# Probabilities transposed in 32x32 blocks by VectorE, and values summed over 32-key blocks in eight tiles of TensorE, in a fused attention and FFN kernel

## The chip, the cores and the metric

The kernel runs on one core of one Trainium2 chip. The metric is device time in microseconds, the median of several runs. The engines are named as in the profile: PE is TensorE (with PEld its weight loads), DVE is VectorE, ACT is ScalarE, POOL is GpSimd, SP is SyncE, which issues most DMAs.

## The reference

There are two parts, and the second takes the first one's output. Attention runs for 8 batches and 8 heads over 576 positions of 64 dimensions, causal by blocks of 64 positions. Its output, 4608 tokens by 512, goes through a bilinear FFN of width 1536.

```python
scores = scale * np.matmul(q, k.transpose(0, 1, 3, 2))
mask = block_i >= block_j            # blocks of 64 positions
scores = np.where(mask, scores, -1000000000.0)
scores = scores - np.max(scores, axis=-1, keepdims=True)
attn = np.exp(scores)
attn = attn / (np.sum(attn, axis=-1, keepdims=True) + 1e-09)
attn_out = np.matmul(attn, v)
...
x = np.ascontiguousarray(attn_out.transpose(0, 2, 1, 3)).reshape(B * S, H * D)
a = x @ w_a
b = x @ w_b
return (a * b @ w_out).astype(np.float32)
```

All inputs are float32. The kernel computes most matmuls as sums of products of float32r parts (a high and a low part of each operand, three products); those of the values, and the scores of the first six pairs, are plain float32.

## The kernel before, in words

Attention is done in 32 pairs of heads, `p`. One turn `s` of the loop at the end of the code below is a *slot*. It walks through the table `SLOT`, whose entries are (generator, pair relative to `s`, number of FFN matmuls that follow). `S1` is a step of `softmax` of pair `s`, `T1` a step of `turn` of pair `s - 1`, and `V_` is `values` of pair `s - 2`. `LAG` is 2, so the loop has two slots more than there are pairs. The FFN matmuls come from `first_pass`, which does 4 of the 12 chunks of the FFN's width for the tokens of batches whose attention is ready; `want` meters them out at 72 a slot, from `MOE_FROM` on, which counts half slots. PE's instructions stand in the order in which this loop emits them; those of the other engines are ordered by a scheduler. In the first slots, where no FFN matmul is ready, `KEEP` puts a few matmuls of zeros behind each step. After attention the other chunks follow in a second pass that this change does not touch.

In a pair, queries are taken in tiles of 128: tile `t` sees `nk[t]` keys, 192, 320, 448 and, for `LAST` = 3, 512. The first and the last block of 64 queries form a tile of their own, `NT` = 4, with 128 keys, the "side". `softmax` computes the scores of `LAST`, of the side and of tile 1 (L383), takes row maxima on DVE (L388, and `nb` at L411), and exponentials on ACT (L391), which also sums them; then scores (2, h) and (0, h) for both heads h, and the same for these. Line 434 makes the reciprocals `rc` of the sums, and POOL multiplies the exponentials by them in place (L438, ten operations a pair). The scores lie in banks of PSUM from a ring of four, `ps_sc`.

`turn` transposes the scaled exponentials on PE, 128 by 128 against an identity matrix, 28 a pair in seven groups (L457), each group into one of two banks `tp`; ACT copies each group to `ah` (L460). `values` multiplies: 12 matmuls a pair (L475) with 128 keys as the contraction, 64 columns of v as weights, one head in each half of the array's columns, sums in `av` and `av0` in the same two banks. DVE copies the sums to `xf` (L484, L485), and the parts `xh` and `xl` for the FFN are made from it. `load_v` loads v of a pair with two DMAs of 160 KB.

The functions that the change touches, and the loop that calls them, with the line numbers of the profile:

Of the kernel before, what the change touches and what calls it, by code (L numbers as in the profile page):

```python
# [26 lines left out]
MOE_FROM = 10.2  # L27
# [27 lines left out]
def attention_then_bilinear_ffn(  # L55
# [212 lines left out]
    ps_sc = psum(right, "ps_sc", 4)  # L268
    ps_t = psum(right, "ps_t", 1)

    ident = const.tile([P, P], F32, name="ident")
    make_identity(nc, ident)
# [14 lines left out]
    SC = slice(P * SIDE_T, P * SIDE_T + BLK), slice(P * SIDE_T + BLK, P * (SIDE_T + 1))  # L287
    NE = 4
    e_bufs, s_bufs = [], []
    for i in range(NE):  # L290
        es = [const.tile([P, ew[t]], F32, name=f"e{i}_{t}") for t in range(NT)]
        for t in range(LAST):
            nc.gpsimd.memset(es[t][:, nk[t]:], 0.0)
        e_bufs.append((es, const.tile([P, P], F32, name=f"e{i}_s")))
# [38 lines left out]
    def load_v(p):  # L333
        b, h, n = pair_of(p)
        vv = heads[p]["v"] = apool.tile([P, 2, NCH + 1, D], F32, tag="v", name=f"v{n}", bufs=3)
        for j in range(2):
            nc.sync.dma_start(vv[:, j], vm[b, h + j])
# [103 lines left out]
    def turn(p):  # L441

        n = pair_of(p)[2]
        heads[p]["a"] = ah = apool.tile([P, 2, NCH, W], F32, tag="ah", name=f"ah{n}")
        for t, hs in [(t, [h]) for t in range(LAST, 0, -1) for h in range(2)] + [(0, [0, 1])]:
            tp = ps_t.tile([P, 4, P], F32, tag="tp", name=f"tp{n}_{t}_{hs[0]}", bufs=2)
            m = min(t + 2, NCH)
            todo = []
            for h in hs:
                es, e_s = e_bufs[(2 * p + h) % NE]  # L450
                todo += [es[t][:, c * P:(c + 1) * P] for c in range(m)]
                if t == SIDE_T:
                    assert m == SIDE
                    todo.append(e_s)
            m = len(todo) // len(hs)
            for c, src in enumerate(todo):
                mark = nc.tensor.transpose(tp[:, c], src, ident)  # L457
            at = slice(hs[0], hs[-1] + 1), slice(m), slice(P * t, P * (t + 1))
            got = tp[:, :len(todo)].rearrange("p (h c) n -> p h c n", h=len(hs))
            nc.scalar.copy(ah[(slice(None), *at)], got)  # L460
            yield mark

    def values(p):
# [5 lines left out]
        av = ps_t.tile([P, W], F32, tag="tp", name=f"av{n}", bufs=2)  # L469
        av0 = ps_t.tile([P, 512], F32, tag="tp", name=f"av0{n}", bufs=2)[:, :BLK]  # L470
# [404 lines left out]
```

## Time and profile before

| what | value |
|---|---|
| median of 3 runs | 1278.81 us |
| runs | 1275.3 to 1279.34 us |
| the profiled execution, as timed | 1277.34 us |
| its span in the trace | 1275.5 us |
| busy: PE, DVE, ACT, POOL | 1229.0, 789.1, 622.8, 353.5 us |
| FFN matmuls start after | 113 us |
| attention ends at about | 650 us |

The profile was taken of one execution. Busy time is time in which an engine had an instruction under way; matmuls overlap, so their busy times are longer than the distance from one start to the next. A line of a group names the line of the kernel, the engine, the operation, output<-input, partitions x elements and the count, then its busy time and the mean of one in nanoseconds, then the idle time before it and what ended most of that.

### The profile page before, as it was taken

To read this page: it belongs to the slowest core of one execution; us is meant where nothing else is said; L and a number is where in the kernel's file an instruction comes from. 1 tells how busy PE (TensorE), PEld (TensorE's weight loads), DVE (VectorE), ACT (ScalarE), POOL (GpSimd) and SP (SyncE) were. 2 spreads that over 40 slices of the span, in tenths; PEclk is the share of its full clock that TensorE was granted. 3 is DMA by queue.
4 is the path that set the end of the run, shared out by engine and by line. 5 is a ranking of instruction groups with operands and counts; after the bars stand their busy time and mean duration, and the time that the engine had idled before them with its cause. 6 is when DMAs were issued, how large, how long until landed. Compare 5 with 4: busy or idle time off the path is not lost.

```text
span 1275.5 us, 22228 instructions
## 1 busy us (share of the span) xinstructions
PE 1229.0 (96%) x8132; PEld 1114.6 (87%) x8132; DVE 789.1 (62%) x1932; ACT 622.8 (49%) x1550; POOL 353.5 (28%) x540
## 2 busy tenths in 40 slices
PE   6789999999999999999999899999999999999998
PEld 4556778888888888888889799999999999999998
DVE  5875444345444454444538999778778677577664
ACT  3656667576675665766645444344344223123210
POOL 2453653554535545355330020120121000000000
PEclk7888999999999999999999999999999999999999
DMA  5342222222222223221133454563578542253131
GB/s 191 107 139 72 71 77 81 96 65 74 80 88 88 65 73 97 70 88 59 35 109 95 151 119 135 153 153 95 142 192 278 161 149 85 65 149 102 47 100 62
DMA packets 68652, 135.66 MB, mean 106 GB/s; under 512 B 7616, under 2 KB 42432, under 8 KB 68544
## 3 DMA queue, kind: packets, MB, share of 16 engines
q1 hardware_dynamic: 57024, 115.37, 28.2%
q0 software_dynamic: 6912, 9.44, 4.7%
q10 hardware_dynamic: 4608, 9.44, 2.2%
q8 instruction: 64, 1.05, 0.3%
q14 instruction: 44, 0.36, 0.1%
HBM read 87.03 MB, written 47.19 MB: 105 GB/s over the span
## 4 chain that ended last, share of the span: by engine, by line
PE 74%; ACT 12%; DVE 10%; issue 3%; DMA 1%; POOL 0%; SPq 0%; ACTq 0%; DVEq 0%
PE pso_z L727 15%; PE ps L223 9%; PE psw_z L681 8%; PE psx_z L681 8%; PE psv_z L681 7%; PE av L475 7%; PE pso L223 6%; PE tp L457 5%; PE s L383 5%; ACT e L391 5%; ACT ah L460 4%; PE psy_z L681 4%; DVE nm L388 3%; ACT e_s L391 2%; PE keep L586 1%
## 5 line engine op out<-in xcount | busy, mean ns | idle before, releaser
L223 PE MATMUL ps<-xh,wab 128*128 128x288 f32 x1024 | 228.8, 305 | 0.0
L727 PE MATMUL pso_z<-h_z,wo 128*128 128x384 f32 x1152 | 203.7, 334 | 2.1 <-DVE u_z L708 2.1
L727 PEld LDWEIGHTS pso_z<-h_z,wo 128*128 128x128 f32 x1152 | 200.2, 188 | 2.5 <-issue 2.3
L438 POOL TENSOR_SCALAR e<-e,rc 128x512 f32<-128x512 f32 (+3 forms) x256 | 150.7, 611 | 161.4 <-DVE rc L434 95.2
L223 PEld LDWEIGHTS ps<-xh,wab 128*128 128x128 f32 x1024 | 168.1, 188 | 8.5 <-issue 5.2
L223 PE MATMUL ps<-xl,wab 128*128 128x288 f32 x512 | 158.0, 309 | 0.0
L460 ACT COPY ah<-tp 128x512 f32<-128x512 f32 x224 | 133.5, 597 | 41.6 <-PE tp L457 41.1
L388 DVE TENSOR_REDUCE nm<-s 128x1 f32<-128x512 f32 (+4 forms) x320 | 147.0, 484 | 9.1 <-PE s L383 6.0
L383 PE MATMUL s<-k,q 64*128 64x512 f32 (+3 forms) x900 | 118.1, 367 | 27.4 <-ACT e L391 24.7
L112 ACT CAST h_z<-u_z 128x384 fp32r<-128x384 f32 x96 | 49.3, 513 | 175.8 <-DVE u_z L706 160.2
L457 PE MATMUL tp<-ident,e 128*128 128x128 f32 x832 | 130.8, 278 | 0.1
L383 PEld LDWEIGHTS s<-k,q 64*128 64x128 f32 x900 | 78.5, 190 | 59.5 <-ACT e L391 42.8
L790 POOL DMA_DIRECT2D part<-pt x48 | 42.7, 1038 | 287.1 <-ACT pt L789 286.4
L681 PE MATMUL psx_z<-xh,wab 128*128 128x384 f32 x384 | 117.6, 342 | 3.7 <-DVE u_z L699 2.0
L681 PE MATMUL psw_z<-xh,wab 128*128 128x384 f32 x384 | 117.4, 341 | 0.0
L681 PE MATMUL psv_z<-xh,wab 128*128 128x384 f32 x384 | 116.2, 338 | 0.0
L223 PE MATMUL pso<-hh,wo 128*128 128x288 f32 x480 | 112.5, 311 | 0.8 <-ACT a L247 0.8
L457 PEld LDWEIGHTS tp<-ident,e 128*128 128x128 f32 x832 | 105.6, 143 | 5.7 <-issue 2.5
L391 ACT ACTIVATE e<-s,nm 128x448 f32<-128x448 f32 (+2 forms) x192 | 101.3, 540 | 19.0 <-DVE nm L388 18.9
L484 DVE COPY xf<-av 128x512 f32<-128x512 f32 x32 | 22.1, 691 | 130.4 <-PE av L475 130.4
L475 PE MATMUL av<-ah,v 128*64 128x64 f32 (+4 forms) x768 | 93.6, 393 | 6.6 <-ACT ah L460 4.5
L223 PEld LDWEIGHTS ps<-xl,wab 128*128 128x128 f32 x512 | 96.4, 188 | 1.6 <-issue 0.4
(114 smaller groups left out, 2323.4 us busy)
## 6 DMA issues: line engine op xcount, KB each, us to landing
xr<-xd SPq DMA_DIRECT2D x48, 384.0 KB, 3.9
raww<-wab SPq DMA_DIRECT2D x24, 512.0 KB, 3.9
v<-vm SPq DMA_DIRECT2D x64, 160.0 KB, 3.4
xd<-xf ACTq DMA_DIRECT2D x32, 288.0 KB, 2.6
part<-ob SPq DMA_DIRECT2D x64, 144.0 KB, 2.0
part<-pt POOLq DMA_DIRECT2D x48, 192.0 KB, 7.3
pt<-part SPq DMA_DIRECT2D x48, 192.0 KB, 3.2
outT<-pt SPq DMA_DIRECT2D x48, 192.0 KB, 3.3
```

Source lines behind the costliest of these rows:

```text
L112: nc.scalar.copy(hi, src)
L223: mm = nc.tensor.matmul(ps, w_, d_, start=(i == 0), stop=(i == n - 1))
L383: mark = nc.tensor.matmul(outs[h], qq[r, q0[t]:q0[t] + P], keys, start=j == 0, stop=j == len(qk) - 1)
L388: nc.vector.tensor_reduce(nm[:, h, t:t + 1], view, axis=AX.X, op=ALU.max, negate=True)
L391: nc.scalar.activation(out, view, AF.Exp, bias=bias, accum_out=sm[:, h, t, :1])
L438: nc.gpsimd.tensor_scalar(ev, ev, rc[:, h, t:t + 1], 1.0, op0=ALU.mult, op1=ALU.mult)
L457: mark = nc.tensor.transpose(tp[:, c], src, ident)
L460: nc.scalar.copy(ah[(slice(None), *at)], got)
L475: mark = nc.tensor.matmul(out[r], v[:, i, c], a[:, i, src, cols], start=start, stop=stop, skip_group_check=True)
L681: nc.tensor.matmul(ps, wt[:, i, iw], j[:, ix], start=start and kp == 0 and i == 0 and j is xh, stop=kp == KP - 1 and i == 1, skip_group_ch ...
L727: nc.tensor.matmul(ps, wt[:, a, osl], b, start=i == 0, stop=i == 3 * len(fs) - 1)
L790: nc.gpsimd.dma_start(part[o * P:(o + 1) * P, ts], t, accum_op=ALU.add)
```

## The change

The identity matrix, `ps_t` and the transposes on PE go. `turn` now transposes with `nc.vector.transpose`, which turns each block of 32 by 32 in its place: 12 instructions a pair, over 3200 columns, into `at`, of which there is one buffer. So `at` holds, for each head, tile and key block of 32, keys on the partitions, but the four groups of 32 partitions are four groups of queries, and each group needs its own copy of v. The host lays v out four times, once for each group of 32 partitions, and `load_v` loads it in one DMA of 1152 KB a pair, two buffers in place of three.

`values` sums over 18 key blocks of 32: for each of them four row groups `i` of 32 partitions, and in each both heads in the two halves of the columns, 144 matmuls a pair in place of 12. Row group i of both heads sums into bank `av[i]`. These four banks come from `ps_sc`, which has six now. In the order of that ring `av[0]` and `av[1]` take the banks of tile 1 and the side, `av[2]` and `av[3]` those of (2, 0) and (2, 1); the next pair's first scores take those of (0, 0) and (0, 1). ACT copies the sums to `xf` in six copies; DVE has none.

`values` of pair s - 1 stands in slot s now, behind the sixth of `softmax`'s eight steps, that of (2, 1), with 14 FFN matmuls behind it, and 7 and 11 more behind the last two steps. `load_v`, `split_qk` and `load_qk` are called at other entries, `MOE_FROM` is 9.6, the loop has one slot more than there are pairs, and `KEEP` counts only at entries with FFN matmuls.

```diff
--- before.py
+++ after.py
@@ -4,7 +4,6 @@
 import concourse.bass as bass
 import concourse.tile as tile
 from concourse import mybir
-from concourse.masks import make_identity
 from concourse._compat import with_exitstack
 
 F32 = mybir.dt.float32
@@ -24,7 +23,7 @@
 CONV_PER_SLOT = 0.88
 CONV0 = 1
 HL_DVE = False
-MOE_FROM = 10.2
+MOE_FROM = 9.6
 FR = 6
 X_EVERY = 48
 OB = 3
@@ -265,11 +264,8 @@
     xpool = pool(left, "xpool", 2)
     const = pool(right, "const", 1, "right")
     apool = pool(right, "apool", 2, "right")
-    ps_sc = psum(right, "ps_sc", 4)
-    ps_t = psum(right, "ps_t", 1)
-
-    ident = const.tile([P, P], F32, name="ident")
-    make_identity(nc, ident)
+    ps_sc = psum(right, "ps_sc", 6)
+
 
 
 
@@ -284,13 +280,12 @@
 
     W = S - BLK
     SIDE, SIDE_T = 3, 1
-    SC = slice(P * SIDE_T, P * SIDE_T + BLK), slice(P * SIDE_T + BLK, P * (SIDE_T + 1))
+    QB = 32
+    NQ, NB = P // QB, S // QB
     NE = 4
     e_bufs, s_bufs = [], []
     for i in range(NE):
-        es = [const.tile([P, ew[t]], F32, name=f"e{i}_{t}") for t in range(NT)]
-        for t in range(LAST):
-            nc.gpsimd.memset(es[t][:, nk[t]:], 0.0)
+        es = [const.tile([P, nk[t]], F32, name=f"e{i}_{t}") for t in range(NT)]
         e_bufs.append((es, const.tile([P, P], F32, name=f"e{i}_s")))
     for i in range(2):
         s_bufs.append(const.tile([P, 2, NT + 1, 2], F32, name=f"sm{i}"))
@@ -332,9 +327,8 @@
 
     def load_v(p):
         b, h, n = pair_of(p)
-        vv = heads[p]["v"] = apool.tile([P, 2, NCH + 1, D], F32, tag="v", name=f"v{n}", bufs=3)
-        for j in range(2):
-            nc.sync.dma_start(vv[:, j], vm[b, h + j])
+        vv = heads[p]["v"] = apool.tile([P, 2, NB, D], F32, tag="v", name=f"v{n}")
+        nc.sync.dma_start(vv, vm[b, h // 2])
 
     def parts_of(p, tag):
         return heads[p].pop(f"{tag}r"), *(heads[p][tag].bitcast(F32R)[:, j] for j in (1, 0))
@@ -441,24 +435,15 @@
     def turn(p):
 
         n = pair_of(p)[2]
-        heads[p]["a"] = ah = apool.tile([P, 2, NCH, W], F32, tag="ah", name=f"ah{n}")
-        for t, hs in [(t, [h]) for t in range(LAST, 0, -1) for h in range(2)] + [(0, [0, 1])]:
-            tp = ps_t.tile([P, 4, P], F32, tag="tp", name=f"tp{n}_{t}_{hs[0]}", bufs=2)
-            m = min(t + 2, NCH)
-            todo = []
-            for h in hs:
+        heads[p]["a"] = at = apool.tile([P, 2, NT + 1, S], F32, tag="at", name=f"at{n}", bufs=1)
+        for t in (*range(LAST, 0, -1), 0):
+            for h in range(2):
                 es, e_s = e_bufs[(2 * p + h) % NE]
-                todo += [es[t][:, c * P:(c + 1) * P] for c in range(m)]
+                nc.vector.transpose(at[:, h, t, :nk[t]], es[t])
                 if t == SIDE_T:
-                    assert m == SIDE
-                    todo.append(e_s)
-            m = len(todo) // len(hs)
-            for c, src in enumerate(todo):
-                mark = nc.tensor.transpose(tp[:, c], src, ident)
-            at = slice(hs[0], hs[-1] + 1), slice(m), slice(P * t, P * (t + 1))
-            got = tp[:, :len(todo)].rearrange("p (h c) n -> p h c n", h=len(hs))
-            nc.scalar.copy(ah[(slice(None), *at)], got)
-            yield mark
+                    nc.vector.transpose(at[:, h, LAST, W:], e_s[:, BLK:])
+                    nc.vector.transpose(at[:, h, NT, :BLK], e_s[:, :BLK])
+                yield None
 
     def values(p):
 
@@ -466,23 +451,23 @@
         t = heads.pop(p)
         hp = h // 2
         xf = xpool.tile([P, S], F32, tag="xf", name=f"xf{n}", bufs=XFB)
-        av = ps_t.tile([P, W], F32, tag="tp", name=f"av{n}", bufs=2)
-        av0 = ps_t.tile([P, 512], F32, tag="tp", name=f"av0{n}", bufs=2)[:, :BLK]
+        av = [ps_sc.tile([P, 512], F32, tag="sc", name=f"av{i}{n}") for i in range(NQ)]
         v, a = t["v"], t["a"]
-
-        def both(out, c, src, cols, start, stop):
-            for i, r in enumerate(rows):
-                mark = nc.tensor.matmul(
-                    out[r], v[:, i, c], a[:, i, src, cols], start=start, stop=stop, skip_group_check=True)
-            return mark
-
-        for c in range(NCH):
-            a0 = max(P * c - BLK, 0)
-            both(av[:, a0:], c, c, slice(a0, W), c == 0, False)
-        both(av[:, W - BLK:], NCH, SIDE, SC[1], False, True)
-        mark = both(av0, NCH, SIDE, SC[0], True, True)
-        nc.vector.tensor_copy(xf[:, BLK:], av)
-        nc.vector.tensor_copy(xf[:, :BLK], av0)
+        for j in range(NB):
+            t0 = min(i for i in range(NT) if QB * j < nk[i] or i == LAST)
+            t1 = NT + (j < BLK // QB)
+            for i in range(NQ):
+                r = slice(QB * i, QB * (i + 1))
+                for h, d in enumerate(rows):
+                    mark = nc.tensor.matmul(
+                        av[i][d, QB * t0:QB * t1], v[r, h, j], a[r, h, t0:t1, QB * j:QB * (j + 1)],
+                        start=j == 0, stop=j == NB - 1, skip_group_check=True)
+        for i in range(NQ):
+            nc.scalar.copy(
+                xf[:, BLK:].rearrange("p (t i q) -> p t i q", i=NQ, q=QB)[:, :, i],
+                av[i][:, :QB * NT].rearrange("p (t q) -> p t q", q=QB))
+        for i in range(BLK // QB):
+            nc.scalar.copy(xf[:, QB * i:QB * (i + 1)], av[i][:, QB * NT:QB * (NT + 1)])
         xs = []
         for j in range(2):
             xh, xl = (xpool.tile([P, HT], F32R, tag=f"x{z}", name=f"x{z}{n}_{j}", bufs=3 * NPAIR) for z in "hl")
@@ -569,11 +554,11 @@
     S_, T_, V_ = softmax, turn, values
 
     S1, T1 = (S_, 0), (T_, -1)
-    SLOT = [(V_, -2, 0), (*S1, 6), (*S1, 5), (*T1, 5), (*S1, 5), (*T1, 5), (*S1, 5), (*T1, 6),
-            (*S1, 6), (*S1, 5), (*T1, 5), (*S1, 5), (*T1, 5), (*S1, 5), (*T1, 5), (*T1, 4)]
+    SLOT = [(*S1, 7), (*T1, 0), (*S1, 6), (*T1, 0), (*T1, 0), (*S1, 6), (*T1, 0), (*T1, 0), (*S1, 6),
+            (*T1, 0), (*T1, 0), (*T1, 0), (*S1, 8), (*S1, 7), (V_, -1, 14), (*S1, 7), (*S1, 11)]
     fill = sum(m for _, _, m in SLOT)
     gens = {}
-    for s in range(NP + LAG):
+    for s in range(NP + 1):
         if s == NP - 1:
             raw = fetch(wab[F1, :, 0], f"w{F1}_0")
         due = 0
@@ -581,15 +566,16 @@
             i += s
             if 0 <= i < NP:
                 mark = next(gens.get((what, i)) or gens.setdefault((what, i), what(i)))
-                for _ in range(KEEP[s] if s < len(KEEP) else 0):
+                for _ in range(KEEP[s] if m and s < len(KEEP) else 0):
                     keep = keep or ps_mm.tile([P, 512], F32, tag="mm", name="keep")
                     nc.tensor.matmul(keep, z[:, :P], z, start=True, stop=True)
-                marks.append(mark)
-            if k == 0 and s < NP:
+                if mark is not None:
+                    marks.append(mark)
+            if what is V_ and s < NP:
                 load_v(s)
-            if k == 9 and s + 1 < NP:
+            if k == 13 and s + 1 < NP:
                 split_qk(s + 1)
-            if k == 9 and s + 2 < NP:
+            if k == 13 and s + 2 < NP:
                 load_qk(s + 2)
             if s >= NP and m and n_conv2 < EARLY:
                 conv2 = conv2 or convert_w(parts(range(F1, F1 + F2)), nc.vector, paced=True, raw=raw)
@@ -856,8 +842,7 @@
     arrays = {
         "qT": flat(np.concatenate([q[:, :, BLK:], q[:, :, :BLK], q[:, :, -BLK:]], axis=2).transpose(0, 1, 3, 2)),
         "kT": flat(k.transpose(0, 1, 3, 2)),
-        "vm": flat(np.concatenate([v[:, :, : NCH * P], v[:, :, :BLK], v[:, :, NCH * P:]], axis=2)
-                   .reshape(B, H, NCH + 1, P, D).transpose(0, 1, 3, 2, 4)),
+        "vm": np.tile(v.reshape(B, H // 2, 2, S // 32, 32, D).transpose(0, 1, 4, 2, 3, 5), (1, 1, 4, 1, 1, 1)),
         "wab": flat(np.stack([wb[:, :, 0::2], wa[:, :, 0::2], wa[:, :, 1::2], wb[:, :, 1::2]], axis=3)
                     .reshape(NF, P, NCC // 2, -1)).view(np.int64),
         "wo": flat(moe_w_out.reshape(NF, P, -1)).view(np.int64),
```

How the instructions stand before and after, at the places of the values and of the reciprocals. On PE before, the values of one pair (heads 4 and 5 of a batch), behind FFN matmuls (`pso`) and ahead of the next scores (`s_0_0`, `s_0_1`):

```order
L223 MATMUL pso_0_3_2795<-hl_0_3_2619,wo_85 128x288
L223 MATMUL pso_0_3_2795<-hh_0_3_2618,wo_85 128x288
L475 MATMUL av_4_2821<-ah_4_2634,v_4_2310 64x512 x2
L475 MATMUL av_4_2821<-ah_4_2634,v_4_2310 64x448 x2
L475 MATMUL av_4_2821<-ah_4_2634,v_4_2310 64x320 x2
L475 MATMUL av_4_2821<-ah_4_2634,v_4_2310 64x192 x2
L475 MATMUL av_4_2821<-ah_4_2634,v_4_2310 64x64 x2
L475 MATMUL av_4_2822<-ah_4_2634,v_4_2310 64x64 x2
L383 MATMUL s_0_0_2852<-k_0_2460,q_0_2463 128x512
```

The last group of PE transposes, into `tp`, stands four FFN matmuls ahead of it. On PE after, the start of the values of one pair, which stand behind 15 FFN matmuls that follow the scores of tiles 2 and 0:

```order
L222 MATMUL pso_0_1_3745<-hh_0_1_3335,wo_81 128x288
L462 MATMUL av_4_3751<-at_4_3648,v_4_3536 64x160 x2
L462 MATMUL av_4_3752<-at_4_3648,v_4_3536 64x160 x2
L462 MATMUL av_4_3753<-at_4_3648,v_4_3536 64x160 x2
L462 MATMUL av_4_3754<-at_4_3648,v_4_3536 64x160 x2
```

There are 72 such rows, four banks in turn, and they end with blocks of 32 columns, again ahead of FFN matmuls:

```order
L462 MATMUL av_4_3754<-at_4_3648,v_4_3536 64x32 x2
L222 MATMUL pso_0_1_3745<-hl_0_1_3336,wo_81 128x288
L222 MATMUL pso_0_1_3745<-hh_0_1_3335,wo_81 128x288
L222 MATMUL pso_0_1_3745<-hh_0_2_3548,wo_83 128x288
L222 MATMUL pso_0_1_3745<-hl_0_2_3549,wo_83 128x288
```

So the values moved from ahead of a pair's first scores to a place between its second scores and the next pair's first, with 32 FFN matmuls behind them. On DVE before, from the reciprocal of one pair to the first maxima of the next (`hf` is the product of the FFN's two halves):

```order
L434 RECIPROCAL rc_0_2850<-rc_0_2850 128x10
L249 TENSOR_TENSOR hf_1_2_3016<-ps_1_1_2_2984,a_1_2_2982 128x288
L249 TENSOR_TENSOR hf_1_3_3152<-ps_1_1_3_3062,a_1_3_3060 128x288
L484 COPY xf_6_3087<-av_6_3088 128x512
L485 COPY xf_6_3087<-av_6_3089 128x64
L388 TENSOR_REDUCE nm_2_3116<-s_2_0_3119 128x1
```

The two copies to `xf` stand there. On DVE after, the same stretch of another pair, from the reciprocal on; behind the last row come `L444`, `L445`, the two of tile 0, one product `hf` and the next pair's first maxima:

```order
L428 RECIPROCAL rc_4_3226<-rc_4_3226 128x10
L442 STREAM_TRANSPOSE at_4_3648<-e_3_101 128x512
L442 STREAM_TRANSPOSE at_4_3648<-e_3_106 128x512
L248 TENSOR_TENSOR hf_0_2_3546<-ps_1_0_2_3367,a_0_2_3365 128x288
L442 STREAM_TRANSPOSE at_4_3648<-e_2_100 128x448
L442 STREAM_TRANSPOSE at_4_3648<-e_2_105 128x448
L442 STREAM_TRANSPOSE at_4_3648<-e_1_99 128x320
L444 STREAM_TRANSPOSE at_4_3648<-e_s 128x64
L445 STREAM_TRANSPOSE at_4_3648<-e_s 128x64
L442 STREAM_TRANSPOSE at_4_3648<-e_1_104 128x320
```

All 12 transposes of a pair now stand between its reciprocal and the next pair's first maxima.

## The prediction

> **What bounds the kernel now.** I read the page first, then the windows of three stages, then the groups by line, and last one slot of the attention stage on the timeline.
>
> ```profile
> span 1275.5 us, 22228 instructions
> PE 1229.0 (96%) x8132; PEld 1114.6 (87%) x8132; DVE 789.1 (62%) x1932; ACT 622.8 (49%) x1550; POOL 353.5 (28%) x540
> PE   6789999999999999999999899999999999999998
> PEclk7888999999999999999999999999999999999999
> PE 74%; ACT 12%; DVE 10%; issue 3%; DMA 1%; POOL 0%; SPq 0%; ACTq 0%; DVEq 0%
> ```
>
> PE is busy for 96% of the span and carries 74% of the chain that ended last; only the first slices show it below nine tenths. So work taken from PE is worth its time after the start, if nothing late takes its place. The slices don't say whether the next engine is close behind; the windows do.
>
> ```profile
> core 0: us, PE busy (x) PEld busy (x) DVE busy (x) ACT busy (x) POOL busy (x), PEclk, DMA share, GB/s
> 5.50:112.90 107.40, 83.85 (x382) 53.81 (x383) 77.98 (x204) 60.36 (x160) 42.69 (x57) 0.79 0.38 130
> 246.01:404.19 158.18, 155.98 (x1232) 133.10 (x1232) 70.76 (x240) 102.99 (x297) 77.14 (x121) 1.00 0.25 79
> 649.60:745.00 95.40, 90.81 (x609) 87.24 (x608) 77.98 (x170) 44.91 (x89) 3.62 (x4) 0.98 0.35 111
> ```
>
> The middle row is eight slots of the attention stage: 158.18 / 8 = 19.77 us a slot, PE busy in 155.98 of them, DVE in 8.85 us a slot, ACT in 12.9. The first row is the start, with no FFN matmuls to fill PE. The last begins where attention is over; the change touches little from there on.
>
> **The change part by part.** *Transposes leave PE.*
>
> ```profile
> L457 PE MATMUL tp<-ident,e 128*128 128x128 f32 x832 | 130.8, 278 | 0.1
> L460 ACT COPY ah<-tp 128x512 f32<-128x512 f32 x224 | 133.5, 597 | 41.6 <-PE tp L457 41.1
> 402.53 0.43 PE L223 MATMUL pso<-hh,wo 128*128 128x288 f32 x2
> 402.80 0.29 PE L223 MATMUL pso<-hl,wo 128*128 128x288 f32 x1
> 402.93 0.60 PE L457 MATMUL tp<-ident,e 128*128 128x128 f32 x4
> 403.29 0.51 PE L223 MATMUL pso<-hh,wo 128*128 128x288 f32 x2
> 403.63 0.29 PE L223 MATMUL pso<-hl,wo 128*128 128x288 f32 x1
> ```
>
> A busy time of pipelined matmuls overlaps its neighbours', so I go by starts. An FFN matmul (line 223) takes 402.80 − 402.53 = 0.27 for two, 0.135 each (0.13 to the next). The group of four transposes holds PE from 402.93 to 403.29, 0.36, and the two matmuls behind it take 0.34 and not 0.27: 0.36 + 0.07, say 0.44. Seven groups a pair: 3.08 us off PE a slot. ACT loses seven copies of 0.597, 4.2 us.
>
> *Values.* Before, 12 matmuls a pair, shown as 24 passes since each float32 matmul is two loads and two passes. Columns for one head: 512 + 448 + 320 + 192 + 64 + 64 = 1600, the two heads in the two column halves. After: 18 blocks x 4 row groups x 2 halves = 144 matmuls, 288 passes, 576 loads and passes; each row group of a head again streams 160·2 + 128·4 + 96·4 + 64·4 + 32·4 = 1600 columns.
>
> ```profile
> 404.20 2.92 PE L475 MATMUL av<-ah,v 128*64 128x512 f32 x24
> 407.06 1.73 PE L383 MATMUL s<-k,q 64*128 64x512 f32 x18
> 404.19:404.21 0.02, 0.01 (x2) 0.01 (x2) 1.00 0.00 0
> ```
>
> The 24 passes hold PE from 404.20 to 407.06, 2.9 us. The last row is a window over the first hundredths of that stretch: two passes have begun within 0.015 us, so the two column halves run side by side. If all eight tiles do, the new values cost A = 2.9 us as now; if the four row groups follow one another, 4 x 2.92 = 11.7. Starting 288 passes at 0.015 each costs at most 4.3. The Trainium skill, "TensorE: Matmul & The Clock Gate", section "Wait — 56ns, not 53.3ns?", says that matmuls never start closer than about 25 ns, however short; as an estimate from that page 288 x 25 ns = 7.2 us, a slot of 22.3 and some 1350 us in all. The window row speaks against it for passes in different tiles.
>
> What else 576 instructions need is to arrive. That is in the transfers.
>
> ```profile
> 0.00:304.35 304.35, 273.69 (x1857) 214.13 (x1858) 167.59 (x504) 188.35 (x526) 139.67 (x225) 0.93 0.31 99
> 0.00:1255.30 1255.30, 1212.41 (x8038) 1098.42 (x8039) 782.57 (x1921) 621.73 (x1548) 353.47 (x540) 0.98 0.36 106
> q8 instruction: 14, 0.23, 0.3%
> q8 instruction: 63, 1.03, 0.3%
> q8 instruction: 1, 0.02, 5.3%
> v<-vm SPq DMA_DIRECT2D x64, 160.0 KB, 3.4
> part<-ob SPq DMA_DIRECT2D x64, 144.0 KB, 2.0
> raww<-wab SPq DMA_DIRECT2D x24, 512.0 KB, 3.9
> ```
>
> The three q8 rows are the instruction queue over 0 to 304.3, over 0 to 1255.3, and in 304.3 to 305.5. Between the first two, 49 packets arrive while PE runs (8038 − 1857) + (8039 − 1858) = 12362 loads and passes: 252 a packet, so this queue feeds PE. With one block in place at the start, 15 x 252 = 3780 were there by 304.35 and 3715 had run; by 1255.3, 64 x 252 = 16128 against 16077. Each time only 50 to 70 are left when the next packet comes. At today's pace of some 0.066 us an instruction these last about 4 us and hide any fetch. In the new values they don't: 576 / 252 = 2.28 packets. Price of one: its transfer alone is 5.3% of the 1.2 us window of 16 engines, 1.0 us; issue to landing of other loads takes 2.0 to 3.9. So supply asks 2.3 to 8.9 us of the values. I take the row of a plain load from memory, 3.4: A = 2.28 x 3.4 = 7.7, bounds 2.9 (columns) and 8.9, and keep 11.7 as a rival.
>
> *Transposes on DVE.*
>
> ```profile
> L484 DVE COPY xf<-av 128x512 f32<-128x512 f32 x32 | 22.1, 691 | 130.4 <-PE av L475 130.4
> L485 DVE COPY xf<-av 128x64 f32<-128x64 f32 x32 | 6.8, 214 | 0.0
> ```
>
> No row shows a DVE transpose. Two copies give (691 − 214) / 448 = 1.065 ns an element and 0.146 us each time. Twelve instructions over 3200 columns: 12 x 0.146 + 3.4 = 5.2 us a pair; twice that if a transpose runs at half pace; nothing below 3.4. The copies leave (0.9): DVE goes from 8.85 to some 13.1 us a slot. They are ordered right behind the reciprocal, ahead of the next pair's first maxima. ACT takes six small copies to xf, some 0.25 each between 0.214 and 0.597: 1.5, so it is 2.7 lighter.
>
> *The rest.* POOL keeps its ten scalings a pair; its memsets are at the start. The load of v is one of 1152 KB a slot in place of 320: at the 79 GB/s now, 0.83 MB more in 20 us is 42 GB/s; the start already moved 130, so I cost it at nothing: it is issued one slot ahead. If that cover went, the values would wait some 7 us for it in a slot.
>
> *Where the values stand.* They now need four banks of the score ring, two of them those of scores (2,0) and (2,1), so PE must wait until ACT has read these.
>
> ```profile
> 400.36 0.22 DVE L434 RECIPROCAL rc<-rc 128x10 f32<-128x10 f32 x1
> 400.67 2.60 POOL L438 TENSOR_SCALAR e<-e,rc 128x512 f32<-128x512 f32 x4 [5.19 <-PE tp L457]
> 403.25 0.72 POOL L438 TENSOR_SCALAR e_s<-e_s,rc 128x128 f32<-128x128 f32 x2
> 403.95 1.85 POOL L438 TENSOR_SCALAR e<-e,rc 128x320 f32<-128x320 f32 x4
> 408.05 1.29 DVE L388 TENSOR_REDUCE nm<-s 128x1 f32<-128x512 f32 x2 [0.17 <-PE s L383]
> 410.46 0.16 DVE L411 TENSOR_REDUCE nb<-nm 64x4 f32<-64x8 f32 x1
> 410.65 0.69 ACT L391 ACTIVATE e<-s,nb 128x512 f32<-128x512 f32 x1 [1.97 <-DVE nb L411]
> 417.78 0.20 ACT L391 ACTIVATION_READ_ACCUMULATOR e<-s,nm 128x1 f32 x1
> ```
>
> From one values to the next PE must pass: the values A; 32 FFN matmuls that stand behind them, 4.2; the next pair's first scores, 1.7 (the x18 row); DVE's first maxima, 408.05 to 410.62, 2.6; ACT's exponentials from 410.65 to the read-out at 417.98, 7.3, which hold two of the old copies, so 6.1 without them; hand-overs 0.2 + 0.2 + 0.1. A slot is A + 15.1. PE's own work is 19.77 − 3.08 − 2.9 + A = A + 13.8, so this loop is longer by 1.3 and PE idles in it: the 40 FFN matmuls between the first scores and the values last 5.3, the maxima and exponentials 8.7 (only the second scores, some 1.5, also fill it). A second loop is POOL's scaling 400.67 to 405.80, 5.1 after the reciprocal, the last transposes to 5.9, maxima 2.6, then 8.6 to the sums and 0.5 to the next reciprocal: 17.6, below it.
>
> *Sum.* Slot 7.7 + 15.1 = 22.8, +3.03 on 19.77. From 112.90 to 649.60 there are 536.7 / 19.77 = 27.1 slots: +82. The first five slots (77.98 of 107.40 busy on DVE) get 4.2 more on DVE each, 21 if all of it shows, and the FFN matmuls start a third of a slot earlier, −7 at best: I take +7, between 0 and +21. At the end the extra slot of the old lag goes: −2. Profiled execution: 1275.5 span, 1277.3 as timed, 0.1% under the median of 1278.8. 1277.3 + 82 + 7 − 2 = 1364 us; against the median 1366. I say 1365.
>
> The Trainium skill, "Runtime: NRT & Kernel Launch", section "Instruction fetch mechanics", says that instructions come in 16 KiB blocks of 256, the next one fetched while the current one runs, and that crossing a block is mostly hidden since instructions issue more slowly than they arrive. The block of 252 agrees. That it stays hidden at this density no row shows; by that rule the first rival below holds.
>
> **The rivals.** (1) *Faster: all eight tiles abreast and the supply keeps ahead.* A is 2.9 to 4.3, the slot 18.0 to 19.4: −1.77 to −0.37 x 27.1, with +5 for the ends 1234 to 1272; at A = 3.2 it is 1242. For it: two passes begin within 0.015 us, and issue is but 3% of the chain. Against: 50 to 70 in hand last a tenth of the time here. It decides at A = 4.5, where the longer loop is 19.6 and the +5 is paid for. (2) *Supply in between*, A from 4.5 to 6: 1277 to 1318. (3) *Row groups don't overlap*, A = 11.7: slot 26.8, +190, 1472. The 18 score passes in two row groups (three products of 512 + 128 + 320 columns for two heads) hold PE 1.73 us; at the FFN's 0.135 for 288 columns they would take 1.35 abreast and 2.70 one after another, so row groups do overlap, though not wholly. (4) *DVE transposes at half pace*: 10.3 a pair; the second loop becomes 10.9 + 2.6 + 8.6 + 0.5 = 22.6, +77, and the start +20: some 1372, whatever A up to 7.5.
>
> **How the numbers follow.** Main 0.47 (A 6 to 8.9: slots 21.1 to 24.0, 1318 to 1397, and to 1440 if the granted clock falls towards the 0.79 of the first stage as PE idles: 72 FFN matmuls of 0.133 would take 2.5 longer a slot). Rival 1: 0.25; 2: 0.12; 3: 0.08; 4: 0.08. Outside 1240 to 1440 lie rival 1 with A under 3.1 (0.08), all of rival 3 (0.08) and a little of the main case, 2 in 10; the main case's own range is 1320 to 1440. Faster by over 0.3% (what a measurement of this kernel can tell from no change): rival 1, 0.25, and a little of 2, 0.26; within 0.3%: 0.04; slower: 0.70.
>
> **What would show it.** PE transposes and the copies from tp gone. One stretch of 288 value passes per slot: its length is A; gaps between passes put down to issue, some 250 instructions apart, with packets of q8 in them, show supply; passes evenly spaced with none show rivals 1 or 3. In front of the values PE waits for ACT's read-out of (2,1), up to 2 us. Slots of 22.8 and PE below 90% in the middle stage; DVE transposes of some 0.69 for 512 columns. I'm wrong if A is under 4.5, if the fetch runs further ahead in a dense stretch than it does now, or if the wait before the values isn't there.

## The result, and the profile after

The changed kernel takes 1320.22 us (median of 4 runs, 1310.5 to 1329.16) against 1278.83: ratio 1.0328, 95% interval 1.0245 to 1.0411. It is slower, as forecast and inside the range, but by 41 us and not by 86. The profiled execution took 1329.16 us, 0.7% over the median, so its sums come out a little high.

From the page of the changed kernel: span, busy times, the granted clock in 40 slices, the chain that ended last, PE's instruction queue and the passes of the values.

```profile
span 1327.4 us, 37261 instructions
PE 1210.3 (91%) x15657; PEld 1139.2 (86%) x15657; DVE 888.2 (67%) x2254; ACT 542.7 (41%) x1518; POOL 353.4 (27%) x524
PEclk8678888898889989788889999999999999999999
PE 68%; DVE 7%; issue 6%; ACT 4%; DMA 1%; DVEq 0%; ACTq 0%
q8 instruction: 122, 2.00, 0.6%
L462 PE MATMUL av<-at,v 32*64 32x64 f32 (+3 forms) x9216 | 152.5, 266 | 71.6 <-issue 65.3
```

Three things are new. PE, 96% busy before, is at 91%. Ahead of passes of the values PE stands idle for 65.3 us that end in "issue", which means that it waited for nothing that the profile shows. And the clock, at 9 in all slices but the first four before, is at 8 or lower in most slices up to the 21st.

Windows with the columns of the prediction's table; the first row is the kernel before, from the fifth pair's values to the last but one's (26 slots), the second the changed kernel, from the fifth pair's to the last's (27).

```profile
129.73:641.72 511.99, 501.82 (x3973) 427.88 (x3974) 231.71 (x785) 332.30 (x957) 250.40 (x392) 1.00 0.24 77
```

```profile
125.37:707.19 581.82, 509.71 (x10450) 470.44 (x10450) 318.78 (x1066) 276.75 (x956) 256.63 (x402) 0.89 0.35 109
```

A slot was 19.69 us and is 21.55, +1.86; 27 of them make 50 of the 51.9 us between the two spans. So what is to be explained lies in the slot. One of them, from the timeline (PE's matmuls, and ACT's last read-out ahead of the values):

```profile
318.75 0.20 ACT L385 ACTIVATION_READ_ACCUMULATOR e<-s,nm 128x1 f32 x1
318.84 3.28 PE L462 MATMUL av<-at,v 32*64 32x160 f32 x234
324.09 0.97 PE L462 MATMUL av<-at,v 32*64 32x32 f32 x54 [1.97 <-issue]
324.99 0.61 PE L222 MATMUL ps<-xl,wab 128*128 128x288 f32 x1
325.40 0.68 PE L222 MATMUL ps<-xh,wab 128*128 128x288 f32 x2
325.88 0.44 PE L222 MATMUL ps<-xl,wab 128*128 128x288 f32 x1
```

The same stretch in windows:

```profile
318.84:322.20 3.36, 3.28 (x235) 3.17 (x235) 1.42 (x5) 2.40 (x9) 0.82 (x1) 1.00 0.20 46
322.20:324.00 1.80, 0.00 (x0) 0.00 (x0) 0.00 (x0) 0.00 (x0) 1.80 (x3) 1.00 0.46 127
324.00:325.00 1.00, 0.91 (x55) 0.84 (x54) 0.00 (x0) 0.08 (x1) 1.00 (x3) 0.72 0.74 235
325.00:328.50 3.50, 3.50 (x18) 3.50 (x18) 2.49 (x5) 2.07 (x9) 3.50 (x8) 0.59 0.75 205
328.50:329.50 1.00, 1.00 (x10) 1.00 (x9) 1.00 (x5) 0.28 (x1) 1.00 (x3) 1.00 0.95 378
```

The values last from 318.84 to 324.99, where the next matmul starts: 6.15 us. 234 passes run, then PE does nothing at all for some 2 us, then the other 54 follow. Behind them the granted clock is 0.59, and FFN matmuls start 0.24 us apart (325.40 to 325.88 for two) in place of 0.13; at 328.5 it is 1.00 again. Over the 27 slots the stretch, measured in this way, lasts 6.7 us on average, from 5.3 to 8.9 by slot; in the kernel before it is 2.85 in all of them. Behind the 28 stretches from the fifth on, FFN matmuls 0.2 to 0.3 us apart stand in rows of 7 to 23, 420 in all, each 0.108 us over: 45 us, 1.6 a slot. The kernel before has such steps in that stage too, 333 of them, but one or two at a time, mostly behind transposes, and at a granted clock of 1.00.

An account of the slot that closes gives to each matmul the time from its start to the next start on PE, over the two windows above:

| us a slot | values | FFN | transposes | scores | sum |
|---|---|---|---|---|---|
| before | 2.85 | 11.02 | 2.48 | 3.34 | 19.69 |
| after | 6.69 | 12.15 | 0 | 2.71 | 21.55 |

The values cost 3.84 more. The FFN's 1.13 more are the 1.6 of the clock less some 0.5 by which transposes held up the matmul behind them. Transposes and scores give back 2.48 and 0.63.

DVE's transposes and ACT's copies, by form:

```profile
L442 DVE STREAM_TRANSPOSE at<-e 128x512 f32<-128x512 f32 x64 | 42.0, 691 | 117.7 <-PE av L462 87.1 <-POOL e L432 25.9 <-POOL e_s L432 4.7
L466 ACT COPY xf<-av 128x128 f32<-128x128 f32 x128 | 25.0, 278 | 121.8 <-PE av L462 57.4 <-POOL e L432 49.9 <-POOL e_s L432 14.5
L470 ACT COPY xf<-av 128x32 f32<-128x32 f32 x64 | 10.1, 232 | 0.0
```

A transpose of 512 columns takes 0.691 us, what a copy took; the twelve, which overlap a little, hold DVE for 4.2 a pair. In 21 cases they wait for the values of the pair before (87.1 us in all), since `at` has one buffer.

### The profile page after: what moved, and what is told of

It is laid out like the page before. It is cut to its first block, busy times and chain, and to the rows that moved or that the text cites. A ratio compares the mean times of both kernels' runs of the same rounds, so it can differ in the third digit from the quotient of the medians.

```text
span 1327.4 us, 37261 instructions
## 1 busy us (share of the span) xinstructions
PE 1210.3 (91%) x15657; PEld 1139.2 (86%) x15657; DVE 888.2 (67%) x2254; ACT 542.7 (41%) x1518; POOL 353.4 (27%) x524
## 4 chain that ended last, share of the span: by engine, by line
PE 68%; DVE 7%; issue 6%; ACT 4%; DMA 1%; DVEq 0%; ACTq 0%
PE pso_z L713 13%; PE ps L222 10%; PE pso L222 8%; PE av L462 8%; PE psw_z L667 7%; PE psv_z L667 7%; PE psx_z L667 7%; PE psy_z L667 4%; PE s L377 3%; DVE nm L382 3%; ACT e L385 3%; DMA xr<-xd 1%; ACT a L246 1%; DMA part<-pt 0%; DVE s L400 0%
## 5 line engine op out<-in xcount | busy, mean ns | idle before, releaser
L462 PE MATMUL av<-at,v 32*64 32x64 f32 (+3 forms) x9216 | 152.5, 266 | 71.6 <-issue 65.3
L462 PEld LDWEIGHTS av<-at,v 32*64 32x64 f32 x9216 | 137.0, 139 | 90.1 <-issue 74.3
L442 DVE STREAM_TRANSPOSE at<-e 128x512 f32<-128x512 f32 (+3 forms) x256 | 124.7, 528 | 117.7 <-PE av L462 87.1
L222 PEld LDWEIGHTS ps<-xh,wab 128*128 128x128 f32 x1024 | 186.2, 210 | 11.4 <-issue 6.2
L382 DVE TENSOR_REDUCE nm<-s 128x1 f32<-128x320 f32 (+4 forms) x320 | 140.9, 477 | 42.1 <-PE s L377 42.0
L222 PE MATMUL ps<-xl,wab 128*128 128x288 f32 x512 | 166.4, 325 | 1.5 <-issue 0.9
L377 PE MATMUL s<-k,q 64*128 64x512 f32 (+3 forms) x900 | 106.7, 361 | 28.2 <-ACT e L385 17.8
L222 PEld LDWEIGHTS ps<-xl,wab 128*128 128x128 f32 x512 | 107.9, 211 | 3.1 <-POOL xl L114 0.8
L114 POOL TENSOR_TENSOR hl<-hf,hh 128x288 fp32r<-128x288 f32 x55 | 44.2, 804 | 223.3 <-ACT hh L111 211.4
L222 PEld LDWEIGHTS pso<-hh,wo 128*128 128x128 f32 x480 | 95.2, 229 | 6.0 <-ACT a L246 5.6
```

What stands on the lines that cost most here:

```text
L114: return lo_eng.tensor_tensor(lo, src, f32(hi), op=ALU.subtract)
L222: mm = nc.tensor.matmul(ps, w_, d_, start=(i == 0), stop=(i == n - 1))
L377: mark = nc.tensor.matmul(outs[h], qq[r, q0[t]:q0[t] + P], keys, start=j == 0, stop=j == len(qk) - 1)
L382: nc.vector.tensor_reduce(nm[:, h, t:t + 1], view, axis=AX.X, op=ALU.max, negate=True)
L442: nc.vector.transpose(at[:, h, t, :nk[t]], es[t])
L462: mark = nc.tensor.matmul(av[i][d, QB * t0:QB * t1], v[r, h, j], a[r, h, t0:t1, QB * j:QB * (j + 1)], start=j == 0, stop=j == NB - 1, skip ...
```

## The experiments

Three theories were set against each other. S: 576 instructions in one stretch outrun their supply, and the idle time behind it halves the clock. C: small tiles lower the clock by themselves. D: the transposes on DVE, behind the values, set the slot.

**Fewer instructions, the same columns (merged).**

```diff
-        for j in range(NB):
+        for j in range(0, NB, 2):
...
-  av[i][d, QB * t0:QB * t1], v[r, h, j], a[r, h, t0:t1, QB * j:QB * (j + 1)],
+  av[i][d, 2 * QB * t0:2 * QB * t1], v[r, h, j], a[r, h, t0:t1, QB * j:QB * (j + 2)],
```

> The values go over every second key block only, but each matmul streams two blocks of columns: 72 matmuls a pair in place of 144, 288 loads and passes in place of 576, and the same 1600 columns for each row group and head. The sums are not the reference's. Theory S (instruction supply and clock): a stretch of 288 instructions meets a late block only about once in eight, the stretch is 2.8 to 3.4 us in place of 5.3 to 8.5, PE is not left idle and the granted clock stays at 0.98 or above after it; slot 17.0 to 17.6, some 1205 to 1240 us. Theory C (tiles of 32 rows lower the clock by themselves, waits or not): the stretch is as short, but the half-clock steps behind it stay; slot about 18.6, 1245 to 1265 us. Theory D (the transposes on DVE set the slot): slot within 1 us of 21.5, 1295 us or more.

Measured: 1218.75 us, ratio 0.9543 (0.9529 to 0.9557). One stretch on the timeline, and a window of some nine slots:

```profile
358.43 3.16 PE L462 MATMUL av<-at,v 32*64 32x320 f32 x144
361.52 0.40 PE L222 MATMUL ps<-xl,wab 128*128 128x288 f32 x1
```

```profile
325.50:480.00 154.50, 144.29 (x2050) 131.63 (x2048) 104.57 (x349) 88.10 (x304) 85.38 (x135) 0.98 0.42 137
```

144 passes of twice the columns hold PE for 3.1 us and, in the slot shown, without a gap, near the 2.9 of the kernel before (four row groups one after another would take 11.7): all eight tiles do run side by side. The clock is 0.98 with the same small tiles, and a slot is 17.6. So columns, tiles and DVE's work do not make the loss: C falls, and D for this form. DVE does all its transposes here too.

**Twice the instructions (double).** Each matmul is issued twice, `for h, d in [*enumerate(rows)] * 2`.

> Each matmul of the values is issued twice, 1152 loads and passes a pair (the sums are doubled, which changes what follows). Theory S: 4.5 blocks of instructions, the first already there, each further one 3.7 us after the one before (1.6 of running and 2.1 of waiting now): a stretch of 14 to 15 us with 3 or 4 waits, 128 passes apart; slot about 30, 1540 to 1580 us. Rival: each instruction simply has its price, so twice today's mean stretch, 12.4 us, slot 27.7, about 1490. Rival: the wait belongs to the stretch (a bank or a semaphore) and comes once: 9.5 us, about 1410.

Measured: 1618.01 us (one run), slots of 30.7. One stretch:

```profile
464.51 5.96 PE L462 MATMUL av<-at,v 32*64 32x160 f32 x288
472.62 2.03 PE L462 MATMUL av<-at,v 32*64 32x96 f32 x128 [2.14 <-issue]
476.36 2.74 PE L462 MATMUL av<-at,v 32*64 32x64 f32 x128 [1.72 <-issue]
479.83 0.73 PE L462 MATMUL av<-at,v 32*64 32x32 f32 x32 [0.73 <-issue]
```

Waits stand 128 passes apart, which with their loads is 256 instructions, and the pieces start 3.74 and 3.47 us apart: a block that PE runs in 2.0 to 2.7 us comes only every 3.6. The instruction queue shows 194 packets in place of 122, 72 more for 2 x 9216 more instructions, 256 each. The stretch (15.6 us on average, 14 to 15 expected) and the slot are near those of S; the total is 38 us over its bound, partly because I counted 27 slots where all 32 pay.

The packets' own times tie the waits to this queue. In the stretch shown, packets land at 471.34, 474.99 and 478.35, and PE goes on at 472.62, 476.36 and 479.83, 1.3 to 1.5 us after each. From the fifth stretch on, every wait of 1.4 us or more inside the values ends in this way: 1.22 to 1.60 us after a packet of the instruction queue has landed in this run (57 waits), 1.23 to 1.56 in the changed kernel (30 waits).

**The big load of v left out (vonce).** v of the first pair is loaded once, and stays.

> v of the first pair is loaded once and used for all pairs, 31 loads of 1152 KB less (the sums are of the wrong v). Theory S with the plain latency of a fetch: the waits inside the values stay at 1.6 to 2.5 us and the time within 0.7% of 1320. Rival (the fetch of instructions is late because the big load of v, issued at the values, is in its way): the waits shrink by half a microsecond or more and the time falls by 15 us or more.

Measured: 1319.45 us, ratio 1.0321 (1.0293 to 1.0349), against 1.0328 for the changed kernel itself.

```profile
343.59 3.28 PE L465 MATMUL av<-at,v 32*64 32x160 f32 x235
348.41 0.76 PE L465 MATMUL av<-at,v 32*64 32x32 f32 x53 [1.55 <-issue]
```

The wait is there without the load: 36 MB less traffic leave the time as it was.

**The stretch alone, in the kernel before (burst).**

```diff
+        for j in range(18):
+            m = 16 * (5 if j < 2 else 4 if j < 6 else 3 if j < 10 else 2 if j < 14 else 1)
+            for g in range(4):
+                r = slice(32 * (g % 2), 32 * (g % 2 + 1))
+                for i, d in enumerate(rows):
+                    nc.tensor.matmul((av, burst)[g % 2][d, :m], v[r, i, j % NCH], a[r, i, j % NCH, W - m:], ...)
```

> The kernel before with one part of the change alone: ahead of its own values of each pair it issues 144 more small matmuls in the new values' count and order (32 rows, 64 columns of weights; half the streamed columns each and two row groups, because only two banks are free), 576 loads and passes. Their results are overwritten, the output stays the reference's. Transposes stay on PE, DVE, ACT and the DMAs are untouched. Theory S: the 288 passes run in some 3.6 us, with one wait of about 2 us for instructions each time, sometimes two, and half clock behind them: 5.5 to 6.5 us plus 1 to 2 a slot, which PE-bound slots pay in full: 27 x 7 to 8, 1465 to 1500 us. Rival (the waits and the lower clock need DVE's and the DMAs' new work): 3.6 a slot and a clock of 1, 1370 to 1385 us.

Measured: 1533.94 us (one run). The timeline of one slot, and a window of some nine:

```profile
404.95 3.41 PE L485 MATMUL av<-ah,v 32*64 32x80 f32 x202
409.74 1.46 PE L485 MATMUL av<-ah,v 32*64 32x32 f32 x86 [1.38 <-issue]
411.13 4.62 PE L476 MATMUL av<-ah,v 128*64 128x512 f32 x24
```

```profile
330.00:600.00 270.00, 250.87 (x4086) 209.49 (x4082) 86.60 (x295) 122.91 (x355) 89.67 (x139) 0.91 0.18 55
```

The wait and the low clock come with the instructions alone: transposes are still PE's, and the old values behind the burst take 4.5 us (411.13 to 415.68) and not 2.9. All 16 waits of 1.4 us or more inside the burst, from the fifth on, end 1.29 to 1.59 us after a packet of the instruction queue has landed. A slot is 8.2 longer, 0.2 over the forecast's upper end, and all 32 pairs pay it, hence 34 us over the bound.

**A second buffer for the transposed probabilities (at2).** Rows are packed 448 columns apart to make room, and v has one buffer.

> The changed kernel with two buffers for the transposed probabilities (rows packed closer, 448 columns apart), so that DVE needn't wait with the transposes until the values are through; one buffer for v, whose load then starts behind the values and has some 14 us. The same instructions otherwise. Theory S (late instructions in the values, then half clock): nothing of this changes, within 0.7% of 1320 us; DVE's wait for the values goes. Theory D (that wait sets the slot): the slot shortens by 2 us or more, below 1275 us.

Measured: 1324.61 us, ratio 1.0380 (1.0338 to 1.0421). What DVE's transposes wait for, first in the changed kernel (255.55 to 424.52), then in this one (330 to 480): line, releaser, total, times, longest.

```profile
DVE at L442 <- PE av L462: 26.1, 7, 4.3
```

```profile
DVE at L443 <- POOL e L433: 19.0, 14, 2.2
```

The wait for the values goes, the time does not (as S forecast, within 0.7% of 1320): in the changed kernel D sets nothing.

**The values in stretches, with FFN matmuls between (split2, split2at2, split3at2).**

```diff
+            if j in (8,):
+                yield None
...
-  (V_, -1, 14), (*S1, 7), (*S1, 11)]
+  (V_, -1, 16), (V_, -1, 0), (*S1, 9), (*S1, 11)]
```

> All 144 matmuls of the values, but in two stretches of 72 with 16 FFN matmuls between them (and 7 and 9 behind the last two steps of softmax in place of 7 and 11). Nothing is left out. Theory S: during the 16 FFN matmuls the next block of instructions arrives; waits of about 2 us inside a stretch all but go (0.1 to 0.7 us a slot left), the clock stays near 1, slot 17.6 to 18.4, 1225 to 1250 us. Theory C: the waits go but not the half-clock steps: slot 19.5 to 20, 1270 to 1290 us. Theory D: the second stretch ends later, so the transposes on DVE start later and the slot grows: 1320 us or more.

> The values in two stretches with 16 FFN matmuls between, as in split2, and two buffers for the transposed probabilities, as in at2. Nothing is left out. In split2 the loop is values 6.4, then transposes and maxima 7.1, exponentials 5.5, hand-overs 0.2: 19.25 us. Reading of it: with the second buffer the transposes start with POOL's scaling some 1.3 to 2.3 us sooner, and the slot falls to 17.2 to 18.2, where PE's own work (13.8 + 3.8 + remaining waits 0.8) is near too: 1225 to 1250 us. Rival: POOL's scaling, which starts behind the reciprocal all the same, sets when the transposes end; slot 18.8 to 19.3, 1265 to 1290 us.

> As split2at2, with the values in three stretches of 48 matmuls and 11 and 10 FFN matmuls between. Theory S: the remaining waits for instructions shrink to half a microsecond a slot or less, but the last stretch ends 0.7 us later; between 10 us faster and 10 us slower than split2at2.

The table that ran in split2 has 9 and 11 behind the last two steps, and not the 7 and 9 that I expected to run. It adds up to 76, which the loop shares out over the 72 of a slot: by the trace 16 FFN matmuls stand between the two stretches and 19 behind them, so 35 lie between the start of the values and the next scores, where the changed kernel has 32. In split2at2 it is the same, in split3at2 and split6 36. These versions so differ from the changed kernel in more than the split.

Measured: split2 1290.7 us, ratio 1.0107 (1.0090 to 1.0124); split2at2 1288.01, 1.0074 (1.0047 to 1.0100); split3at2 1284.63, 1.0055 (1.0034 to 1.0076). From split2, one slot (PE, DVE, ACT) and a window:

```profile
383.65 2.49 PE L462 MATMUL av<-at,v 32*64 32x160 f32 x144
388.39 1.80 PE L462 MATMUL av<-at,v 32*64 32x96 f32 x144
390.32 2.75 DVE L442 STREAM_TRANSPOSE at<-e 128x512 f32<-128x512 f32 x5 [2.04 <-PE av L462]
397.46 0.69 ACT L385 ACTIVATE e<-s,nb 128x512 f32<-128x512 f32 x1 [3.54 <-DVE nb L405]
402.90 1.35 PE L462 MATMUL av<-at,v 32*64 32x160 f32 x59
```

```profile
325.50:480.00 154.50, 143.29 (x3106) 127.23 (x3106) 91.98 (x308) 79.61 (x279) 77.04 (x120) 1.00 0.42 127
```

S is right on the waits and the clock (1.00; 18 FFN steps in slow rows in place of 420), and that is worth 30 us against the changed kernel. But the total isn't the 1225 to 1250 that I gave with S; it lies at the edge of the 1270 to 1290 that I gave with C, whose low clock is not there. I read the slot shown as bound by D now: from values to values 19.25 us pass, by way of the transposes, which start when the second stretch is through, the maxima, and the exponentials at 397.46. The second buffer then should have brought 1225 to 1250 and hardly helped (its rival, 1265 to 1290, came in), so that reading isn't shown. In split2at2 (330 to 480) another wait stands in PE:

```profile
PE ps L222 <- DVE hf L248: 8.8, 8, 1.8
```

The transposes stand among the products `hf` in DVE's order, and these free PE's FFN banks; no run took that order alone away. In split3at2, over the same window, it is also the exponentials that PE waits for ahead of the values:

```profile
PEld av L467 <- ACT e L386: 7.3, 7, 1.0
```

**FFN matmuls moved ahead of the values (split3b, split2b), and six stretches (split6).**

> split3at2 with five FFN matmuls moved from behind the values to ahead of them (45 ahead, 27 from the first stretch on; FFN start at 9.85 half slots). Nothing is left out. If the loop first scores, maxima, exponentials, values, FFN matmuls sets the slot (PE waited up to 1.0 us a slot for the exponentials ahead of the values), it loses 0.7 us a slot: 1260 to 1272 us. If the product hf on DVE, queued behind maxima and transposes, holds PE's next FFN matmuls, nothing is gained: 1278 to 1292.

> split2at2 with five FFN matmuls moved from behind the values to ahead of them (45 ahead, 27 from the first stretch on, 14 of them between the two; FFN start at 9.7 half slots). Nothing is left out. In the slot read from split2at2 PE waits for hf and not for the exponentials: within 10 us of split2at2, 1278 to 1298; if the loop over the values sets it, 1265 to 1275.

> As split3at2, with the values in six stretches of 24 matmuls and 4 FFN matmuls between them (40 FFN matmuls ahead, 32 from the first stretch on as in the changed kernel; FFN start at 9.75 half slots). Nothing is left out. Theory S: 576 instructions of values and 40 of FFN matmuls between now take some 3.8 + 2.7 = 6.5 us, 2.4 blocks; a block each 2.7 us where one needs 3.7, so a wait of about 1 us once a slot is left, and no half clock; slot 18.5 to 20, 1265 to 1295 us. Rival (changing between values and FFN matmuls costs more than the waits that it saves, 0.36 us a change in split2): 4 changes more than split2at2, 1.4 us a slot, 1310 us or more.

Measured: split3b 1309.1 us (ratio 1.0251, 1.0228 to 1.0274), outside both forecasts; split2b 1289.8 (1.0112, 1.0089 to 1.0136), no change on split2at2; split6 1296.79 (1.0145, 1.0105 to 1.0186), just over the 1265 to 1295 of S and under its rival's 1310. In split3b, over 330 to 480, and the passes of split6 with the idle time ahead of them:

```profile
PE ps L222 <- DVE hf L248: 11.5, 3, 4.0
```

```profile
L467 PE MATMUL av<-at,v 32*64 32x64 f32 (+3 forms) x9216 | 201.4, 269 | 24.2 <-ACT e L386 20.5 <-issue 1.8 <-DMA v<-vm 1.5
```

By the trace split2b has 27 FFN matmuls from the first stretch on, 8 less than split2at2, and split3b 27, 9 less than split3at2; I had meant to move five. In split3b the moved matmuls wait for `hf`, up to 4 us at once. In split6 the waits for instructions are down from 65.3 to 1.8 us and no row of slow steps is left, and still a slot is 20.2: PE waits 20.5 us in all for the exponentials, and each change between values and FFN matmuls costs some 0.4 us by an estimate from split2, where the passes of the two stretches stand 2.49 us apart and 16 FFN matmuls take 2.13 (13.8 + 3.8 of passes + 5 x 0.4 + 0.6 = 20.2). No version that computes the whole sum beats the kernel before; split3at2 comes nearest.

## Why the prediction was right in sign and wrong in size

*Transposes off PE, 3.08.* About right: 2.48 by the table, and some 0.5 that the matmuls behind them lost. Merged fits: it has 17.6 us a slot, and 19.69 − 3.08 − 2.9 + 3.6 (its mean stretch) is 17.3.

*The values, A = 7.7: 6.7 measured.* This step failed in size. I charged 2.28 packets with a whole latency each, and let nothing of it overlap with the passes. The packets are there (256 instructions each, 122 in all), and one of them can be placed: in the slot shown, the instruction queue's only packet in a window of 321.5 to 322.5, which starts at 321.77 and has landed at 322.73, is

```profile
q8 instruction: 1, 0.02, 6.0%
```

while PE stands from 321.9 to 324.09. The price of 3.4 for a block was near: in double the pieces start 3.5 to 3.7 us apart. But the next block is there or on its way while PE runs the one before. The place of the wait shows it. In the 12th to the 25th stretch there is one wait of over 1.5 us, behind 247 passes at first and 163 at last, 6 or 7 earlier in each slot, and none 128 passes ahead of it; in the 26th and 27th there are two, 128 passes apart. So the first border in a stretch costs nothing, and a later one only what 128 passes (1.6 us) don't cover of some 3.6. With 288 passes there are (288 − 128) / 128 = 1.25 such borders on average, of 1.5 to 2.5 us mostly and up to 3.7, on top of 3.6 to 3.8 of passes: 5.5 to 6.9. That is the low end of my main case (A 6 to 8.9, 1318 to 1397), and the rival "supply in between" (A 4.5 to 6, up to 1318) lies just below it.

The Trainium skill, "Runtime: NRT & Kernel Launch", section "Instruction fetch mechanics", has the block of 256 and the fetch beside execution right, and both show here; its "mostly hidden" doesn't hold where 256 instructions run in 1.6 us. The floor of 25 ns between matmuls that the Trainium skill, "TensorE: Matmul & The Clock Gate", section "Wait — 56ns, not 53.3ns?", states doesn't hold for passes in different tiles: 234 start in 3.1 us, 13 ns apart.

*The loop A + 15.1: it doesn't bind.* This is the second step that failed, and with it the wait before the values that was to show it. PE waited for ACT only 21.2 us ahead of values in the whole run:

```profile
  issue: 139.6, 97
  ACT e L385: 21.2, 38
```

(who ended the idle time ahead of line 462, loads and passes together). Two terms were too large. The maxima begin 1.0 us after the first score and not behind all of them:

```profile
309.83 1.73 PE L377 MATMUL s<-k,q 64*128 64x512 f32 x18
310.82 1.29 DVE L382 TENSOR_REDUCE nm<-s 128x1 f32<-128x512 f32 x2 [2.55 <-PE s L377]
313.43 0.69 ACT L385 ACTIVATE e<-s,nb 128x512 f32<-128x512 f32 x1 [3.05 <-DVE nb L405]
```

From the first score to the first exponential 3.6 us pass where I counted 1.7 + 0.2 + 2.6 + 0.2; and the exponentials up to the read-out at 318.95 take 5.5, not 6.1. That makes A + 13.4, just under PE's own A + 13.8. The rows in the prediction had it: scores from 407.06, maxima from 408.05, the first exponential at 410.65, again 3.6 us.

*The clock: only in the upper end of the range, 1.6 us a slot measured.* I had bound it to PE idling ahead of the values. It falls behind the values, after the wait for instructions. It falls with them in burst too, and stays at 0.98 to 1.00 in the windows of merged, split2, split2at2, split3at2 and split6; in split2b and split3b it is 0.92 and 0.93 from 330 to 480, with waits for `hf` of up to 3 and 4 us. So the slot that I forecast at 22.8 was 21.55 by other terms: 1.0 less for A, 1.6 more for the clock, and 1.8 less for all the rest, where the loop had 15.1 and 21.55 − 6.69 − 1.6 = 13.3 was left. That 1320 still fell into the main case's bounds is in part luck, since the clock, which the sum had at nothing, made up for most of the loop: without its 45 us the time would be some 1275.

*DVE.* 5.2 forecast, 4.2 measured; ACT's copies 1.5 forecast, 4 x 0.278 + 2 x 0.232 = 1.6. Rival 4 is out. v's load is hidden (vonce). Start and end: +5 forecast, some +2 left of the span.

## What to carry to other kernels

Count instructions beside columns: where PE would run 256 loads and passes in less than the 3.6 us in which the next 256 came here, the rest is idle time from the second border on, and it appears as a wait for "issue" that no engine ends. The wait costs more than its length if the clock falls behind it, so put long matmuls between short ones before judging such a layout. And when one wait is taken away, look at once for the loop that was level with it: here several seem to lie within 2 us of each other.

## What was not expected of the hardware

Passes in different tiles start 13 ns apart, loads between them. The half clock came after a stretch of 5 to 9 us that held 1.5 to 4.9 us of idle time, 28 times in 28, and not after most split stretches, with waits of 0.5 to 1.4 us and full-size matmuls between; after waits of 1.9 and 2.4 us in split2 it came again, though not after two more of 1.9. The trace's record of the granted clock shows more. In the changed kernel all its changes lie on one grid with steps of 3.41 us, and a low lasts whole steps. Around the slot shown, with the columns of the windows above:

```profile
317.62:321.03 3.41, 3.41 (x163) 3.25 (x166) 2.36 (x8) 3.41 (x11) 0.00 (x0) 1.00 0.00 0
321.03:324.45 3.42, 1.45 (x140) 1.33 (x125) 0.27 (x2) 0.21 (x1) 3.08 (x4) 1.00 0.52 126
324.45:327.86 3.41, 3.41 (x48) 3.35 (x34) 1.85 (x4) 1.77 (x9) 3.41 (x9) 0.50 0.71 193
327.86:331.27 3.41, 3.41 (x27) 3.16 (x27) 3.21 (x11) 0.78 (x2) 2.34 (x4) 1.00 0.78 305
```

From 115 to 700 us, each of the 27 full-clock steps of the grid that a half-clock step followed had PE busy for 21 to 62% of it; of the 109 that none followed, 107 had it busy for 77% or more, the other two for 61 and 69%. So here the idle share of such a step goes with the half clock. The border isn't sharp: in at2, five steps at 52 to 58% were not followed by it, and burst has falls behind steps that the profile shows as busy for 70% and more. What exactly is counted stays open. The Trainium skill, "TensorE: Matmul & The Clock Gate", section "HAM oscillation — how this bites in real kernels", gives idle gaps of more than about 3.4 us as the abstract rule; here gaps of 2 us were enough.
